# Batched Wo rows and residual assembly in small steps around V and Wo, x blocks transposed by DMA, VectorE side work in the Wo stretch

## The chip, the cores and the metric

One core of a Trainium2 chip. The metric is device time in microseconds (us), lower is better. Before the change: 902.95 us, median of 3 runs (901.86 to 905.41). A *step* below is the time from the first exponential of one recurrent segment to that of the next, read from the timeline; there are 63 such intervals between 64 segments. *Position* 0 to 3 is the step's number modulo 4, and four steps make one block of 128 rows of x.

## The reference

Layer norm, then attention with a recurrent memory over 64 segments of 32 rows (32 heads, 8 memory rows made anew by each segment), a residual, then layer norm and a gMLP mixer with a second residual.

```python
for s in range(n_seg):                       # 64, each needs the memory of the one before
    h = concat([mem, xs], axis=1)            # 8 + 32 rows
    q, k, v = h @ Wq, h @ Wk, h @ Wv         # 32 heads of 128
    p = softmax(where(mask, q @ k.T * scale, -1e9))
    o = (p @ v) @ Wo
    mem, out_s = o[:, :M], o[:, M:]
h  = x + concat(outs)
h2 = h + gmlp(layernorm(h))                  # w_in, w_sp (2048 x 2048), w_out
```

## The kernel before

The last 8 rows of each segment don't depend on the order in which the memory runs (the name `X` marks them): their Q, K and V for all segments of a chunk are made in *extra groups*, one group in each of steps 0 to 47, and their output rows are multiplied by Wo apart, four segments at a time (`WoX`). The parts that the change touches, in the program order of one step; `late` is work that is emitted early in the next step, behind the memory rows:

```python
for s in range(NSEG):
    j4, rb = s % 4, s // 4
    QK(s, QKP[0], (0, 1))
    if s > 0:
        mem_out(s - 1, 1)                    # memory rows back into hT
        for f in late: f()                   # <- evictions, statistics, ...
    # ... QK pieces, ScalarE evacuation, VectorE stream transposes, scores, exp, V ...
    for f in xs[:2]: f()                     # extra group, first half of its matmuls
    PV_half(s, 0); PV_half(s, 1)
    for f in xs[2:4]: f()                    # second half
    if j4 == 3 and rb > 0:
        F_group(rb - 1, WXB)                 # assembles 128 rows of the residual
        WoX_scatter(rb - 1, WXB)
    # ... cT evictions ...
    if j4 == 3 and rb > 0:
        F_add(rb - 1, WXB)
    Wo(...); part_evac(...); mem_out(s, 0); mask_dve()     # cut
    late += xs[4:]                           # extra group's eviction, VectorE
    if j4 == 1 and 2 <= rb + 2 < RB:
        ln_inplace(0)                        # x block rb+2: statistics, rstd, apply
    if j4 == 2 and 2 <= rb + 2 < RB:
        xT(0, FBK)                           # four PE transposes
        late.append(lambda rb=rb: ring_copy(rb + 2, FBK))  # ScalarE
    if s + 1 < NSEG and s >= 3:
        WoX_mm((s + 1) // 4 - 1, (j4 + 1) % 4)             # 8 matmuls in every step
        if j4 == 2:
            late.append(lambda rb=rb: WoX_evac(rb - 1))    # ScalarE
    if j4 == 0 and rb >= 2:
        xn2_apply(rb - 2, rb % 2); xn2_store(rb - 2, rb % 2)
    if s == 3 * CK:                          # step 48
        sp(lambda e: e.dma_start(w_in2, winr[:, :, FH:F]), ...)   # 896 KB for the tail
```

Every odd step also has a DMA transpose of 64 rows of w_sp and its 256 KB store (`wT_piece`). All DMA is issued by one queue, SP, in program order (in the trace before, the 896 KB load went out at 567.68 us, behind the store of `xn2` at 567.30 that stands ahead of it).

## Time and profile before

| stretch | us |
|---|---|
| start, to the first exponential | 58.3 |
| step 0 | 15.4 |
| steps 1 to 15 | 155.8 |
| steps 16 to 47 | 331.3 |
| steps 48 to 62 | 152.3 |
| rest: last segment and gMLP tail | 190.7 |

From the profile page of the kernel before: busy time of each engine, and shares of the chain of waits by engine.

```profile
PE 870.1 (96%) x22506; PEld 537.7 (59%) x22513; DVE 499.6 (55%) x1231; ACT 451.9 (50%) x1274; POOL 156.4 (17%) x403
...
PE 88%; DVE 7%; issue 2%; ACT 1%; POOL 1%; DMA 0%; SPq 0%; ACTq 0%
```

The shortest steps of each position in steps 16 to 47 are 9.96, 10.45, 10.43 and 10.39 us. At the end of position 1 the chain of waits of the kernel before leaves PE (columns: start, duration, engine, tile, line, count):

```profile
327.97 0.10 PE f_ps L648 x8
...
328.26 0.53 DVE f_ps L509
328.80 0.60 DVE f_st L353
...
329.42 0.19 DVE f_mv L354
...
329.69 0.23 POOL f_rs L355
...
330.00 0.58 POOL f_rs L357
...
330.60 0.41 DVE f_xn L363
331.01 0.60 DVE f_arena L416
331.61 0.36 DVE f_QT L491
...
332.71 0.83 PE f_ps L573 x12
```

L509 is the mask copy, L353 to L363 the normalisation of an x block with its detour over GpSimd, L416 the extra group's eviction. The stream transpose of Q (L491) that PE will need stands behind all of it in VectorE's order.

In the last 16 segments there are no extra groups, and the chain of the kernel before leaves PE ahead of PV and ahead of Wo (L627):

```profile
561.89 0.69 DVE f_V_sb L584
562.58 0.30 DVE f_E_sb L559
562.89 0.34 DVE f_V_sb L584
...
563.98 0.30 ACT f_cT L612
...
564.33 1.80 PE f_ps L627 x56
```

One step later, the same chain has a piece that no engine explains: "issue", time in which PE waited for nothing that the profile shows.

```profile
574.28 0.29 PE f_ps L627 x3
574.57 1.40 issue
575.97 1.69 PE f_ps L627 x53
```

### The profile page before, as it was taken

What the parts mean: (1) busy time and instruction counts of PE and PEld (TensorE: products, weight loads), DVE (VectorE), ACT (ScalarE), POOL (GpSimd) and SP (SyncE); (2) the same over time, 40 slices, a digit from 0 to 9 for tenths busy, and PEclk for the clock granted to TensorE, in tenths of its full rate; (3) what the DMA queues carried; (4) which work ended last, traced back from release to release, by engine and by line L of the source; (5) the groups of instructions that cost most, each with busy time, mean ns of one, the idle gap of its engine ahead of it and who ended that gap; (6) DMA issues with size and microseconds to landing.
All of it is one profiled execution on the core that took longest, in us unless ns stands there. A gap on an engine that the chain in (4) does not pass through costs nothing.

```text
span 903.8 us, 48903 instructions
## 1 busy us (share of the span) xinstructions
PE 870.1 (96%) x22506; PEld 537.7 (59%) x22513; DVE 499.6 (55%) x1231; ACT 451.9 (50%) x1274; POOL 156.4 (17%) x403
## 2 busy tenths in 40 slices
PE   7989999999999999999999999899999999999997
PEld 6665666566666666666666666556566544434443
DVE  3435556566666656566666666555655554543343
ACT  2335566555566655666555666556665655300000
POOL 1501111121211211112212112111111122100000
PEclk9999999999999999999999999999999999999999
DMA  9971211322203020312113120404123590022101
GB/s 327 377 211 45 62 54 42 71 62 57 72 27 68 22 71 21 76 34 55 53 42 58 35 69 22 123 26 93 41 48 63 176 275 1 1 99 76 59 12 37
DMA packets 99586, 71.50 MB, mean 79 GB/s; under 512 B 62248, under 2 KB 84912, under 8 KB 99376
## 3 DMA queue, kind: packets, MB, share of 16 engines
q1 hardware_dynamic: 99376, 68.32, 27.6%
q8 instruction: 178, 2.92, 1.3%
q14 instruction: 32, 0.26, 0.1%
HBM read 39.46 MB, written 18.61 MB: 64 GB/s over the span
## 4 chain that ended last, share of the span: by engine, by line
PE 88%; DVE 7%; issue 2%; ACT 1%; POOL 1%; DMA 0%; SPq 0%; ACTq 0%
PE f_ps L472 21%; PE f_ps L627 13%; PE f_ps L573 11%; PE f_ps L1012 11%; PE f_ps L405 7%; PE f_ps L424 3%; PE f_ps L592 3%; PE f_ps L677 3%; PE f_ps L974 3%; PE f_ps L1005 3%; PE f_ps L1083 3%; PE f_ps L539 2%; DVE f_V_sb L584 2%; PE f_ps L598 1%; PE f_ps L519 1%
## 5 line engine op out<-in xcount | busy, mean ns | idle before, releaser
L472 PE MATMUL f_ps<-f_arena,f_hT 128*32 128x512 bf16 (+1 forms) x5120 | 239.9, 337 | 0.1
L472 PEld LDWEIGHTS f_ps<-f_arena,f_hT 128*32 128x32 bf16 x5120 | 125.8, 96 | 94.2 <-ACT f_hT L656 23.0
L483 ACT ACTIVATE f_Tst<-f_ps 128x512 bf16<-128x512 f32 (+1 forms) x320 | 148.5, 512 | 56.7 <-PE f_ps L472 47.1
L573 PE MATMUL f_ps<-f_arena,f_hT 128*32 128x256 bf16 (+1 forms) x3072 | 143.5, 308 | 0.5
L627 PE MATMUL f_ps<-f_arena,f_cT 128*32 128x256 bf16 x4096 | 133.5, 275 | 6.4 <-ACT f_cT L612 4.6
L563 POOL TENSOR_TENSOR f_E_sb<-f_R_sb,f_E_sb 128x64 bf16<-128x64 f32 x128 | 48.0, 375 | 409.3 <-ACT f_R_sb L555 409.3
L627 PEld LDWEIGHTS f_ps<-f_arena,f_cT 128*32 128x32 bf16 x4096 | 95.6, 96 | 29.2 <-ACT f_cT L612 11.5
L491 DVE STREAM_TRANSPOSE f_QT<-f_Tst 128x256 uint32<-128x256 uint32 x128 | 56.9, 445 | 89.5 <-ACT f_Tst L483 89.5
L1012 PE MATMUL f_ps<-f_arena 128*128 128x512 bf16 x448 | 103.0, 384 | 2.4 <-DVE f_arena L1018 1.6
L639 ACT ACTIVATE f_part<-f_ps 128x256 bf16<-128x256 f32 x128 | 49.0, 383 | 92.7 <-PE f_ps L627 92.7
L584 DVE TENSOR_SCALAR f_V_sb<-f_ps 128x512 bf16<-128x512 f32 (+1 forms) x128 | 70.6, 551 | 41.1 <-PE f_ps L573 41.1
L614 DVE TENSOR_SCALAR f_cT<-f_ps 128x160 bf16<-128x160 f32 (+1 forms) x192 | 61.0, 374 | 39.3 <-PE f_ps L598 39.3
L1012 PEld LDWEIGHTS f_ps<-f_arena 128*128 128x128 bf16 x448 | 43.9, 99 | 57.2 <-DVE f_arena L1018 2.6
L573 PEld LDWEIGHTS f_ps<-f_arena,f_hT 128*32 128x32 bf16 x3072 | 68.8, 96 | 14.5 <-ACT f_Tst L483 1.8
L612 ACT ACTIVATE f_cT<-f_ps 128x160 bf16<-128x160 f32 (+1 forms) x192 | 53.0, 349 | 40.0 <-PE f_ps L598 40.0
L405 PE MATMUL f_ps<-f_hTe,f_arena 128*128 128x128 bf16 x1024 | 70.4, 223 | 0.1
L491 DVE STREAM_TRANSPOSE f_KT<-f_Tst 128x128 uint32<-128x128 uint32 (+1 forms) x192 | 63.8, 338 | 3.1
L405 PEld LDWEIGHTS f_ps<-f_hTe,f_arena 128*128 128x128 bf16 x1024 | 58.9, 99 | 9.2 <-issue 7.1
L551 ACT ACTIVATE f_R_sb<-f_ps 128x160 f32<-128x160 f32 x128 | 38.8, 303 | 35.8 <-PE f_ps L544 35.8
L654 DVE CAST f_hT<-f_ps 128x16 bf16<-128x16 f32 x63 | 11.0, 175 | 78.2 <-PE f_ps L648 78.2
L1018 DVE TENSOR_TENSOR f_arena<-f_ps,f_arena 128x512 f32<-128x512 f32 x28 | 19.3, 691 | 59.5 <-PE f_ps L1012 59.5
L559 DVE TENSOR_TENSOR f_E_sb<-f_R_sb,f_E_sb 128x160 bf16<-128x160 f32 x128 | 45.6, 356 | 0.0
(103 smaller groups left out, 1089.5 us busy)
## 6 DMA issues: line engine op xcount, KB each, us to landing
wT_d<-f_wst SPq DMA_DIRECT2D x32, 256.0 KB, 2.5
f_arena<-wT_d SPq DMA_DIRECT2D x32, 256.0 KB, 4.3
f_arena<-in_A_Wq_dram SPq DMA_DIRECT2D x4, 1024.0 KB, 8.6
f_arena<-in_A_Wv_dram SPq DMA_DIRECT2D x4, 1024.0 KB, 14.3
f_arena<-in_A_Wk_dram SPq DMA_DIRECT2D x4, 1024.0 KB, 14.5
f_arena<-in_A_Wo_dram SPq DMA_DIRECT2D x4, 1024.0 KB, 8.5
f_Vx<-vext_d SPq DMA_DIRECT2D x64, 64.0 KB, 2.7
f_xn<-in_A_x_dram SPq DMA_DIRECT2D x17, 128.0 KB, 2.5
```

The costliest lines, as they stand in the source:

```text
L405: pe(lambda e, h=h, dc=dc, hh=hh: e.matmul(ps[:, bank, hh * 128:(hh + 1) * 128], lhsT=ws[:, dc, h * DH:(h + 1) * DH], rhs=hTe[:, ck % 3, d ...
L472: pe(lambda e, dc=dc, c=c, rhs=rhs: e.matmul(ps[32 * c:32 * c + 32, bank, 0:32 * nh], lhsT=hT[:, sl, dc, :], rhs=rhs, start=(dc == 0), sto ...
L483: act(lambda e: e.activation(out=st_.rearrange("p (hp i r) -> p hp i r", i=32, r=2), in_=ps[:, bank, 0:64 * np_].rearrange("p (hp r i) -> ...
L491: dve(lambda e: e.transpose(out=dst, in_=src), reads=tok, writes=[(nm, b, k) for k in halves(b, p0, np_)])
L563: pool(lambda e: e.tensor_tensor(out=ev, in0=rv, in1=ev, op=ALU.mult), reads=[("R", b), ("Ex", b)], writes=[("Ex", b)])
L573: pe(lambda e, dc=dc, c=c, c0=c0: e.matmul(ps[32 * c:32 * c + 32, bank, 0:w], lhsT=hT[:, sl, dc, :], rhs=w_v[:, dc, c0:c0 + w], start=(dc ...
L584: dve(lambda e: e.tensor_scalar(out=dst, in0=src, scalar1=VSC, scalar2=None, op0=ALU.mult), reads=[PB(bank)], writes=tok)
L612: act(lambda e: e.activation(out=dst, in_=src, func=ACT.Copy, scale=UNSC), reads=[PB(PVB[c])], writes=tok)
L614: dve(lambda e: e.tensor_scalar(out=dst, in0=src, scalar1=UNSC, scalar2=None, op0=ALU.mult), reads=[PB(PVB[c])], writes=tok)
L627: pe(lambda e, h=h, g=g, i=i, b=b, c=c: e.matmul(ps[32 * g:32 * g + 32, bank, 0:d1 - d0], lhsT=cTh[:, i, 8:40], rhs=w_o[:, h, d0:d1], star ...
L639: act(lambda e: e.activation(out=part[:, s % 8, d0:d1], in_=ps[:, bank, 0:d1 - d0], func=ACT.Copy), reads=[PB(bank)], writes=[("part", s % ...
L1012: pe(lambda e: e.matmul(ps[:, bank, 0:TB], lhsT=z2[:, sc, fb * 128:(fb + 1) * 128], rhs=wTb[tb % 2][:, :, sc, :], start=(sc == 0), stop=(s ...
```

## The change

Its intent: take the x transposes off PE, take VectorE's normalisation and evictions out of the way of the stream transposes, and move the WoX, F and scatter matmuls to where PE has room.

```diff
+    def x_flip(j, i, dst, tok):                  # store to DRAM, DMA transpose back
+        sp(lambda e: e.dma_start(xs_d[i], t), ...)
+        sp(lambda e: e.dma_start_transpose(out=dst, in_=xs_d[i]), ...)
+    def ring_fill(rb):                           # VectorE copy into hT
...
+        nw1, nw4 = ((1, 1, 0, 0)[j4], (2, 2, 0, 2)[j4]) if s < 3 * CK else ((4, 4, 0, 0)[j4], 0)
+        if j4 == 3 and rb > 0:
+            WoX_scatter(rb - 1, WXB)
+        for f in wq[:nw1]:                       # WoX in pieces of 4 matmuls, ahead of PV
+            f()
...
-        if j4 == 3 and rb > 0:
-            F_group(rb - 1, WXB)
-            WoX_scatter(rb - 1, WXB)
...
         if j4 == 3 and rb > 0:
             F_add(rb - 1, WXB)
+            late += xs[4:]
+            late.append(lambda rb=rb: h_done(rb - 1))
+        else:
+            for f in xs[4:]:                     # extra group's eviction, ahead of Wo
+                f()
...
-        late += xs[4:]
+        if j4 == 0 ...: late.append(lambda: ln_stats(0))
+        if j4 == 0 ...: late.append(lambda rb=rb: ring_fill(rb + 1))
         if j4 == 1 and 2 <= rb + 2 < RB:
-            ln_inplace(0)
+            late.append(lambda rb=rb: (ln_apply(0), x_flip(0, rb, ...)))
-        if j4 == 2 and 2 <= rb + 2 < RB:
-            xT(0, FBK)
-            late.append(lambda rb=rb: ring_copy(rb + 2, FBK))
-        if s + 1 < NSEG and s >= 3:
-            WoX_mm((s + 1) // 4 - 1, (j4 + 1) % 4)
+        if s + 1 < NSEG:
+            if j4 == 3:
+                wq.extend(... 8 pieces of WoX_mm ...)
+            elif j4 == 2 and rb > 0:
+                F_group(rb - 1, WXB)
+            for f in wq[:nw4]:                   # behind Wo
+                f()
...
-        if j4 == 0 and rb >= 2:
-            xn2_apply(rb - 2, rb % 2)
-            xn2_store(rb - 2, rb % 2)
+        if j4 == 1 and rb >= 2: late.append(... xn2_apply, xn2_store ...)
```

(Cuts and shortened conditions are marked by dots.)

More of the change, by code (lines that the diff above doesn't have):

```diff
@@ L255, in fast_path @@
     h_d = nc.dram_tensor("h_d", [RB, 128, D], BF, kind="Internal").ap()
+    xs_d = nc.dram_tensor("xs_d", [RB + 1, 128, D], BF, kind="Internal").ap()
     wT_d = nc.dram_tensor("wT_d", [S // 64, 128, RB, 64], BF, kind="Internal").ap()
@@ L378, in slot @@
         return s % NSLOT
+    def x_flip(j, i, dst, tok):
+        t, rd = xbuf(j)
+        sp(lambda e: e.dma_start(xs_d[i], t), reads=rd, writes=[("xs", i)])
+        sp(lambda e: e.dma_start_transpose(out=dst, in_=xs_d[i]), reads=[("xs", i)], writes=[tok])
+    def ring_fill(rb):
+        src = xn[:, 1, :].rearrange("p (dc s c) -> p s dc c", dc=DC, s=4, c=SEG)[:, :, :, 0:XM]
+        s0 = slot(4 * rb)
+        dve(lambda e: e.tensor_copy(out=hT[:, s0:s0 + 4, :, M:32], in_=src), reads=[("xn", 1)], writes=[("hTx", rb % 3)])
     def ring_copy(rb, bank):
@@ L671, in load_h, with WoX_mm @@
         sp(lambda e: e.dma_start(hbuf[:, rb % 2, :], xr[:, rb, :]), writes=[("h", rb % 2)])
-    def WoX_mm(rb, qr):
-        for bg in range(8):
+    def WoX_mm(rb, qr, bgs=range(8)):
+        for bg in bgs:
             b, g = bg // 4, bg % 4
@@ L821, in fast_path @@
     lastop = {}
+    wq = []
     qx_copy(0)
@@ L834, in fast_path @@
         if s == 1:
-            load_xe(3, 1)
+            load_xe(3, 7)
         QK(s, QKP[0], (0, 1))
@@ L884, in fast_path @@
             lastop["x"] = em.by_eng["pool"][-1]
+        late = []
+        nw1, nw4 = ((1, 1, 0, 0)[j4], (2, 2, 0, 2)[j4]) if s < 3 * CK else ((4, 4, 0, 0)[j4], 0)
[3 more added lines that the diff above has]
+            f()
+        del wq[:nw1]
         xs = gx.pop(0) if gx else []
-        late = []
         for f in xs[:2]:
@@ L912, in fast_path @@
         part_evac(s, OB2, OC, D)
-        if j4 == 3 and rb > 0:
-            late.append(lambda rb=rb: h_done(rb - 1))
-        late += xs[4:]
+        if j4 == 0 and 2 <= rb + 2 < RB:
+            late.append(lambda: ln_stats(0))
+        if j4 == 0 and 2 <= rb + 1 < RB:
+            late.append(lambda rb=rb: ring_fill(rb + 1))
         if j4 == 1 and 2 <= rb + 2 < RB:
-            ln_inplace(0)
+            late.append(lambda rb=rb: (ln_apply(0), x_flip(0, rb, xn[:, 1, :].rearrange("p (dc c) -> p dc c", dc=DC), ("xn", 1))))
+        if s == 2:
+            late.append(lambda: ln_stats(7))
         if s == 3:
-            ln_inplace(1)
-        if j4 == 2 and 2 <= rb + 2 < RB:
-            xT(0, FBK)
-            late.append(lambda rb=rb: ring_copy(rb + 2, FBK))
-        if s == 5:
-            xT(1, FBK)
-            late.append(lambda: xe_copy(3, FBK))
-        if s + 1 < NSEG and s >= 3:
-            WoX_mm((s + 1) // 4 - 1, (j4 + 1) % 4)
-            if j4 == 2:
-                late.append(lambda rb=rb: WoX_evac(rb - 1))
-        if s + 1 == NSEG:
+            late.append(lambda: (ln_apply(7), x_flip(7, RB, hTe[:, 0, :, :], ("hTe", 0))))
+        if j4 == 1 and rb >= 2:
+            late.append(lambda rb=rb: (xn2_apply(rb - 2, rb % 2), xn2_store(rb - 2, rb % 2)))
+        if j4 == 1 and rb > 0:
+            late.append(lambda rb=rb: WoX_evac(rb - 1))
+        if s + 1 < NSEG:
+            if j4 == 3:
+                wq.extend(lambda rb=rb, k=k: WoX_mm(rb, k // 2, range(4 * (k % 2), 4 * (k % 2) + 4)) for k in range(8))
+            elif j4 == 2 and rb > 0:
+                F_group(rb - 1, WXB)
+            for f in wq[:nw4]:
+                f()
+            del wq[:nw4]
+            assert not wq or j4 in (0, 3)
+        else:
             for f in late:
```

## The prediction

> **What bounds it now.** The page gives PE 96% busy, and the chain of waits is 88% PE. The 64 recurrent steps take 654.8 us of the 903.8 (first to last step's first exponential, timeline). [...]nearly all slices read 9, yet step lengths by position in a block of four, steps 16 to 47, are 9.96, 10.46, 10.45 and 10.39 us.
>
> - Position 1 alone has a chain that leaves PE, for VectorE and GpSimd (statistics 0.60, aggregate 0.19, GpSimd 0.23 and 0.58, apply 0.41, then the 0.60 eviction of the extra QK/V group), which hold up the first Q/K stream transposes. Cost 0.49 us.
> - Position 2: four PE transposes of x (0.33 us in the chain), and two extra ScalarE evictions (0.48, 0.60) ahead of the first Q/K evacuation (about 0.15 more).
> - Position 3: F and scatter matmuls, 8 in about 0.54 us, 0.43 net.
> - Each step from 3 on also has 8 WoX matmuls (0.43 us) between Wo and QK.
>
> The last 16 steps have no extra groups: the chain runs V evictions and normalisation on VectorE (0.69, 0.30, 0.34) and a 0.30 cT eviction on ScalarE, so PE idles about 0.4 us before PV and about 0.3 before Wo. These steps still take 9.95 us.
>
> **What changes.**
>
> - Removed: the PE transposes (13 blocks x 0.33 = 4.3 us), the ring evictions on ScalarE, and the normalisation chain waiting on itself in front of the stream transposes: about 0.5 us in each of 13 blocks = 6.5 us. The position 2 ScalarE delay, 0.15 x 12 = 2 us.
> - Moved: WoX and F/scatter matmuls, count unchanged, to position 3, 0 and 1 after Wo or between V and PV. For steps 16 to 47 PE work per block becomes 4 x 9.53 + 1.73 (32 WoX) + 0.43 (8 F/scatter) = 40.3 us against 41.2 to 41.7: 1.0 us per block, more in steps 0 to 15 where PV already waits a little. In the last 16 steps they land where PE idled: about 0.4 us a block, plus the transposes, 2 us in all. The extra eviction moves to VectorE's idle Wo stretch.
> - Added: 13 stores of 128 KB (similar ones land in 2.2 us), 13 DMA transposes (similar: 3.1 us), 12 VectorE copies[...]. Steps of slack hide them.[...]
>
> Sum: about 6 us in steps 0 to 15, 7 in 16 to 47, 2 at the end: 15 us. The gMLP tail (184 us) is unchanged.
>
> **Prediction: 888 us, 883 to 894 (8 in 10).** Chances: faster by over 2% 0.27, within 2% 0.72, slower by over 2% 0.01.
>
> **Right if:** position 1's chain is PE only; no PE transposes before the tail; steps near 10.15, 10.15, 9.75, 10.15 us in steps 16 to 47; ScalarE idle grows; VectorE copies of x stay off the chain. **Wrong if:** Wo with no WoX behind it exposes the memory-row eviction (0.1 us a step at least in steps 48 to 63); the 16 matmuls before PV exceed the hole in the last 16 steps; VectorE work queued after the mask copy delays the stream transposes again; or PE instruction-fetch waits (4.1 and 1.4 us in this trace) move.

## The result, and the profile after

892.8 us median of 4 runs (891.3 to 895.6), beside 902.4 us of the kernel before (4 runs). The ratio is 0.989, 95% interval 0.986 to 0.993: faster by about 1.1%, inside the predicted range. A ratio is the mean time of one kernel's fast runs over that of the other's of the same rounds, so it is not quite the ratio of the medians quoted. The unaltered changed kernel was run twice more as a control: 893.3 us against 907.1 (ratio 0.985, interval 0.982 to 0.988) and 894.8 against 904.1 (0.988, interval 0.983 to 0.992). The changed kernel repeats better than the kernel before, whose medians in the four sessions were 902.4, 906.4, 907.1 and 904.1; the prediction set out from its fast end.

From the page of the changed kernel:

```profile
PE 854.8 (96%) x22453; PEld 524.2 (59%) x22453; DVE 504.3 (57%) x1245; ACT 449.2 (50%) x1259; POOL 156.3 (18%) x403
...
PE 94%; DVE 3%; issue 2%; ACT 1%; DMA 0%; POOL 0%; SPq 0%
```

The share of PE in the chain rose from 88 to 94%, GpSimd left it and VectorE's share went from 7 to 3%: in steps 16 to 47 of this trace the chain is PE and 1.3 us of "issue", so the stalls that the prediction named there are gone. The chain of waits of the changed kernel at the end of position 1, the place shown of before at 328 us:

```profile
480.52 1.66 PE f_ps L638 x56
482.18 0.05 PE f_ps L659 x8
482.23 0.24 PE f_ps L638 x8
482.47 0.43 PE f_ps L688 x8
482.90 0.43 PE f_ps L483 x7
483.33 0.04 PE f_ps L659 x7
483.36 3.11 PE f_ps L483 x72
486.47 0.09 PE f_ps L530 x16
```

It is PE from Wo (L638) over the memory rows (L659), WoX (L688) and QK (L483) to the scores (L530). The shortest steps of the positions in steps 16 to 47 are now 10.07, 10.07, 9.77 and 10.07 us, 39.98 a block against 41.23 before (each sum from the four shortest steps). But not all steps are so short. By stretch, in us, in the traces of the kernel before and of three runs of the changed one (its first, and the two controls):

| stretch | before | changed, three traces |
|---|---|---|
| step 0 | 15.4 | 12.6, 11.0, 11.0 |
| steps 1 to 15 | 155.8 | 153.2, 152.8, 154.1 |
| steps 16 to 47 | 331.3 | 323.8, 327.5, 327.2 |
| steps 48 to 62 | 152.3 | 153.7, 151.6, 150.4 |
| all steps | 654.8 | 643.2, 643.0, 642.8 |

The steps gained 11.6 to 12.0 us where 15 were predicted. That gain is flattered: the trace of the kernel before is of a run of 905.5 us, 2.5 above its median, and its step 0 holds a 4.1 us piece of "issue" with 3.41 us at half clock after it. Eight blocks of 39.98 would make 319.8 us for steps 16 to 47; the three traces stand 4.0 to 7.7 above that, and in the kernel before the same difference was 1.5 (331.3 less 8 x 41.23). So part of what the order gained came back as irregular waits.

In the last 16 segments the chain still leaves PE. V evictions (L595) hold 6.2 us of it in this trace, where they held 15.6 before, and cT evictions 4.5 (3.6 before). One piece is new: with no WoX behind Wo, the eviction of the memory rows (L665) lies between Wo and QK, 0.19 us in 11 of the 15 steps.

```profile
556.36 0.10 PE f_ps L659 x7
...
556.48 0.19 DVE f_hT L665
...
556.71 0.61 PE f_ps L483 x7
```

The largest irregular wait is in step 48. The chain of waits of the changed kernel there:

```profile
549.29 0.86 PE f_ps L688 x16
550.15 0.13 PE f_ps L603 x3
550.28 2.15 issue
552.42 0.26 PE f_ps L603 x13
...
553.38 2.98 PE f_ps L638 x52
```

PE stopped for 2.15 us between two matmuls of the same group (L603), and then the Wo matmuls (L638) took 2.98 us, where they take 1.66 above. Busy time and granted clock (PEclk, the third value from the end) of the changed kernel in stretches of that step show why:

```profile
550.00:552.40 2.40, 0.28 (x7) 0.10 (x3) 0.00 (x0) 0.00 (x0) 0.57 (x2) 1.00 0.11 22
552.40:554.00 1.60, 1.22 (x52) 0.98 (x56) 0.91 (x3) 0.83 (x3) 0.00 (x0) 0.57 0.46 174
554.00:556.00 2.00, 2.00 (x44) 1.55 (x40) 0.04 (x1) 0.38 (x1) 0.40 (x1) 0.50 0.48 98
```

After the wait PE ran at half clock; the trace's clock records put it at 552.61 us for 3.41 us. Step 48 took 13.58 us, 3.5 more than the typical 10.1 of its position in the last 16 segments.

What does PE wait for? "issue" only says that no semaphore explains it. The trace also records DMA packets of kind "instruction": 178 packets of 16,384 bytes on one queue. Each "issue" wait of PE in the recurrent part was held against the last such packet that ended before the wait did:

```
wait of PE (us)     last instruction packet   wait ends after packet's end
 59.96 to  62.14     59.54 to  60.86          1.28
156.53 to 156.88    154.43 to 155.35          1.52
216.26 to 217.15    214.78 to 215.71          1.44
389.74 to 390.20    387.00 to 388.82          1.38
550.28 to 552.42    549.90 to 550.95          1.48
582.28 to 582.89    580.39 to 581.44          1.46
all 18 waits of the changed kernel             1.28 to 1.56
all 9 waits of the kernel before               1.21 to 1.67
```

Packets come about every 4 us (median 3.90 us from start to start in the trace before, 3.89 in the changed kernel's), so a wait that had nothing to do with them would end anywhere from 0 to 4 us after one. All 27 end 1.2 to 1.7 us after, and so do 263 of the 264 waits in the other twelve traces (1.16 to 1.93 us). From this I take it that PE was waiting for its own instructions. The kernel before has 178 such packets too, and PE ran 45,019 matmuls and weight loads in it: about 253 a packet, an estimate from these two counts, with every packet taken as PE's, of the instructions that one brings (a *block* below). Between 56 and 730 us either trace has 164 packets, so 9 waits before and 18 after mean that most blocks came without one; the waits there add up to 6.8 us before and 10.4, 8.9 and 9.6 us in the three traces of the changed kernel. "Fetch waits" below are this sum: PE's idle gaps over 60 ns that are put down to "issue".

This sum is a floor. The trace draws a matmul of Wo 273 ns long, though 56 of them start within 1.6 us, so a late start shows as a gap only beyond the end of the one before. Against the starts of PE's instructions in the shortest step of the same position, the first trace stands thus: of the 4.0 us that steps 16 to 47 take above the shortest, 3.6 arise 1.1 to 1.75 us after the end of a packet, where the gaps show 1.3; in the first control, 6.8 of 7.6, where they show 3.5. So nearly all of that excess goes with the fetch.

In step 48 the packet before this one had started at 543.02; the next started only at 549.90, 6.9 us later. Between 546 and 550 us DMA moved 308 GB/s. The timelines of the SP queue, first of the kernel before, then of the changed one, show what had moved (start, duration of the issue):

```profile
567.68 0.50 SPq L940 DMA_DIRECT2D f_arena<-in_B_w_in_dram  x1
```

```profile
542.92 1.81 SPq L963 DMA_DIRECT2D f_arena<-in_B_w_in_dram  x1
...
545.32 1.27 SPq L732 DMA_TRANSPOSE f_wst<-in_B_w_sp_dram  x1
```

The line of the 896 KB load of w_in isn't in the diff. Before, SP reached it only in step 49, because the store of `xn2` ahead of it in SP's order waited for VectorE until 567.3 us; there it came with the 1.40 us piece of "issue" shown above, in a step 49 of 11.51 us. The change moved that store elsewhere, and the load went out 25 us earlier, ahead of step 48's exponentials: SP issued it at 542.92 us, and the first of these started at 547.22.

### The profile page after: what moved, and what is told of

Its sections match the earlier page's. It is cut to its first block, busy times and chain, and to the rows that moved or that the text cites. A ratio compares the mean times of both kernels' runs of the same rounds, so it can differ in the third digit from the quotient of the medians.

```text
span 890.5 us, 48841 instructions
## 1 busy us (share of the span) xinstructions
PE 854.8 (96%) x22453; PEld 524.2 (59%) x22453; DVE 504.3 (57%) x1245; ACT 449.2 (50%) x1259; POOL 156.3 (18%) x403
## 4 chain that ended last, share of the span: by engine, by line
PE 94%; DVE 3%; issue 2%; ACT 1%; DMA 0%; POOL 0%; SPq 0%
PE f_ps L483 26%; PE f_ps L638 14%; PE f_ps L584 12%; PE f_ps L1035 11%; PE f_ps L416 7%; PE f_ps L435 3%; PE f_ps L688 3%; PE f_ps L997 3%; PE f_ps L1028 3%; PE f_ps L603 3%; PE f_ps L1106 3%; PE f_ps L550 2%; PE f_ps L530 1%; PE f_ps L609 1%; DVE f_V_sb L595 1%
## 5 line engine op out<-in xcount | busy, mean ns | idle before, releaser
L483 PE MATMUL f_ps<-f_arena,f_hT 128*32 128x512 bf16 (+1 forms) x5120 | 241.3, 337 | 1.5 <-issue 0.5
L483 PEld LDWEIGHTS f_ps<-f_arena,f_hT 128*32 128x32 bf16 x5120 | 125.1, 96 | 96.4 <-ACT f_hT L667 22.9
L638 PE MATMUL f_ps<-f_arena,f_cT 128*32 128x256 bf16 x4096 | 134.7, 275 | 9.2 <-ACT f_cT L623 6.2
L638 PEld LDWEIGHTS f_ps<-f_arena,f_cT 128*32 128x32 bf16 x4096 | 92.8, 96 | 34.2 <-ACT f_cT L623 13.1
L595 DVE TENSOR_SCALAR f_V_sb<-f_ps 128x512 bf16<-128x512 f32 (+1 forms) x128 | 70.6, 552 | 41.4 <-PE f_ps L584 41.4
L584 PEld LDWEIGHTS f_ps<-f_arena,f_hT 128*32 128x32 bf16 x3072 | 69.2, 96 | 14.7 <-issue 2.2
L502 DVE STREAM_TRANSPOSE f_KT<-f_Tst 128x128 uint32<-128x128 uint32 (+1 forms) x192 | 65.7, 343 | 4.2
L543 ACT ACTIVATE f_E_sb<-f_ps 128x224 bf16<-128x224 f32 x128 | 45.1, 353 | 0.0
```

Of the source, the lines that this page charges most:

```text
L483: pe(lambda e, dc=dc, c=c, rhs=rhs: e.matmul(ps[32 * c:32 * c + 32, bank, 0:32 * nh], lhsT=hT[:, sl, dc, :], rhs=rhs, start=(dc == 0), sto ...
L502: dve(lambda e: e.transpose(out=dst, in_=src), reads=tok, writes=[(nm, b, k) for k in halves(b, p0, np_)])
L584: pe(lambda e, dc=dc, c=c, c0=c0: e.matmul(ps[32 * c:32 * c + 32, bank, 0:w], lhsT=hT[:, sl, dc, :], rhs=w_v[:, dc, c0:c0 + w], start=(dc ...
L595: dve(lambda e: e.tensor_scalar(out=dst, in0=src, scalar1=VSC, scalar2=None, op0=ALU.mult), reads=[PB(bank)], writes=tok)
L638: pe(lambda e, h=h, g=g, i=i, b=b, c=c: e.matmul(ps[32 * g:32 * g + 32, bank, 0:d1 - d0], lhsT=cTh[:, i, 8:40], rhs=w_o[:, h, d0:d1], star ...
```

## The experiments

Theory A: the predicted gain is real as a sum of PE work and stalls removed, and what is missing is PE waiting for its instructions behind DMA traffic. Rivals are named with each run. The first four kernels ran on one chip (before: 906.4 us), the other eight on another (before: 907.1 and 904.1 us). All are correct except the one made wrong.

### One part undone: x transposed on PE again

```diff
-  ring_fill(rb + 1) on VectorE; x_flip(...) after ln_apply(0)
+  if j4 == 2 ...: xT(0, FBK); late.append(lambda rb=rb: ring_copy(rb + 2, FBK))
```

> The changed kernel with one part undone: x blocks transposed by PE in position 2 and evicted by ScalarE again, batching and VectorE placement kept. Theory A (gain is the sum of PE work and stalls removed; the excess over it is PE waiting for its instructions behind DMA traffic): position 2 goes from 9.77 to about 10.10 us, 13 x 0.33 = 4.3 us on the sum of the shortest steps (626.7 to about 631), fetch waits fall a little from 10.4 us, so 1 to 4 us slower than the changed kernel (892.8), about 895. Rival B (the DMA transposes cost what was missing from the predicted gain): as fast as the changed kernel or faster, fetch waits under 6 us.

Measured: 894.0 us, ratio 0.986 (interval 0.981 to 0.990). The shortest step of position 2 went from 9.77 to 10.18 us, the others stayed at 10.07. From the groups of PE's instructions of this kernel in steps 16 to 31, the transposes are back:

```profile
L374 PE MATMUL f_ps<-f_ident,f_xn 128*128 128x128 bf16 x16 | 1.6, 222 | 0.0
```

Fetch waits were 8.2 us. So the order pays 0.4 us a block for PE transposes, as theory A had it, but the whole kernel was no slower than the changed one by a margin that the runs resolve (0.986 against 0.985 to 0.989), and all its steps took 645.3 us against 643. By that difference the transposes on DMA would be worth about 2 us, not the 4.3 of their PE work, but this compares one trace with three, and fetch waits alone move steps 16 to 47 by 3.7 us between traces of the same kernel: the worth in time is not resolved. Rival B is not supported: waits did not fall under 6.

### One part undone: WoX in every step again

```diff
-  pieces of WoX ahead of PV and behind Wo; F_group in position 2, scatter ahead of PV
+  WoX_mm((s + 1) // 4 - 1, (j4 + 1) % 4) in every step; F_group and scatter ahead of Wo in position 3
```

> The changed kernel with one part undone: 8 WoX matmuls after Wo in every step, F and scatter before Wo in position 3, as before. Theory A: PE work per block is the same, so the block of four in steps 16 to 47 stays at 40.0 us within 0.2 (10.4 in position 3, less elsewhere), and the last 16 steps go from about 39.6 to 39.8 a block: 1 us slower in all, about 894. Rival (batching is what pays): block back to 40.5 or more, 6 us slower in all, about 899.

Measured: 896.9 us, ratio 0.989 (0.984 to 0.994). The shortest steps are 9.96, 9.96, 9.96 and 10.39, 40.27 a block, 0.3 more than the changed kernel's 39.98; steps 16 to 47 sum to 327.4 us, the same as two of the three traces of the changed kernel. In the last 16 segments steps went back to 9.95 us each. The bound of 0.2 us was missed by 0.1: four matmuls ahead of PV cost a step 0.11 us (10.07 less 9.96), not the 0.21 that their piece of the chain shows. They start 1.89 us into the step; the extra group's matmuls, which stand ahead of PV in both kernels, start only at 2.00 where they follow V directly, so half of the cost falls into a hole that was there. Why they start no earlier is not shown. By time it lies between theory and rival, and its ratio is that of the recorded result (0.989), so the runs don't resolve it.

### One part undone: the extra group's eviction late again

```diff
-            for f in xs[4:]: f()     # ahead of Wo
+            late += xs[4:]           # behind the mask copy, in the next QK stretch
```

> The changed kernel with one part undone: the eviction of the extra group goes back behind the mask copy in the QK stretch in all positions. Theory A: VectorE has about 2 us between the mask copy and the first stream transpose, and the queued work (eviction 0.6, statistics 0.8[...]) just fits: position 1's chain stays PE only, at most 0.2 us a block, under 2 us in all, 893 to 895. Rival (the place of the eviction is what pays): VectorE back in position 0 or 1's chain by 0.4 us or more a block, 5 us or more slower, 898 or more.

Measured: 898.3 us, ratio 0.990 (0.985 to 0.994). The time is in the rival's range and the mechanism is not: the shortest block is 39.98 us, the same as the changed kernel's. VectorE's timeline at the end of position 0 in this kernel (in brackets: idle time before, and its releaser):

```profile
480.77 0.68 DVE L427 CAST f_arena<-f_ps 128x512 bf16<-128x512 f32 x1
481.37 0.69 DVE L354 BATCH_NORM_STATS2 f_st<-f_xn 128x6 f32<-128x512 bf16 x1
482.09 0.18 DVE L355 BATCH_NORM_AGGREGATE f_mv<-f_st 128x2 f32<-128x6 f32 x1
482.19 0.23 DVE L389 COPY f_hT<-f_xn 128x384 bf16<-128x384 bf16 x1
482.83 0.45 DVE L502 STREAM_TRANSPOSE f_QT<-f_Tst 128x256 uint32<-128x256 uint32 x1 [0.42 <-ACT f_Tst L494]
```

The eviction (L427), statistics and copy (0.23 us) all fit, and VectorE still idles 0.42 us for ScalarE before the stream transpose. Fetch waits were 13.4 us here, 3.6 of them in step 0, which took 15.6 us. This profile is of the slowest of the four runs, and its span is 8.7 us above the changed kernel's first: 5.6 in the steps, of which 3.0 in step 0 (that wait, with 6.8 us at half clock around its end), 1.3 before them and 1.8 after. So fetch waits are part of the extra time; why they should be more in this kernel stays open. The control is on another chip, and by ratio the kernel is no slower than the recorded result (0.989). Moving this eviction ahead of Wo, one part of the change, is thus not shown to pay.

### The suspected cost taken away: no w_sp transposes (wrong result)

```diff
-        if s % 2 == 1 and s // 2 < NWT:
-            wT_piece(s // 2)          # 32 DMA transposes and stores of 256 KB
```

The tail loads w_sp untransposed, in pieces of the same size, hence the wrong result.

> The changed kernel without the 32 DMA transposes of the spatial weight and their stores; the tail loads the weight untransposed, so the result is wrong on purpose. Theory A (PE's instruction fetch is held up behind bursts of DMA, mostly these): the fetch waits of PE between 56 and 730 us fall from 10.4 to 3 us or less, no half-clock stretch, and it is 7 to 12 us faster than the changed kernel (881 to 886). Rival C (the waits come from the change's own DMAs, or from PE issuing faster than instructions can be brought): waits stay at 8 us or more, at most 3 us faster.

Measured: 888.8 us, ratio 0.981 (0.977 to 0.985). Waits of PE in this kernel (us in total, times, longest):

```profile
PE f_ps L603 <- issue: 2.9, 4, 1.0
PE f_ps L435 <- issue: 1.7, 2, 1.5
...
PE f_ps L638 <- issue: 1.2, 4, 0.6
```

Fetch waits were 7.0 us, not 3 or less, and all 17 of them again end 1.27 to 1.59 us after an instruction packet. Theory A was right in kind and too strong in size: the transposes are one source of traffic in front of the fetch, worth about 4 us of time (888.8 against 893, the latter from other sessions), not the only one. Step 48, which had no transpose beside its load here, still took 11.66 us, with a wait of 0.96 us. Step 9 is telling: 11.0 to 11.8 us in the changed kernel's traces, 9.95 here.

### The control, and three edits against it

> The changed kernel unaltered, on the chip that the next three run on, as their control. 892 to 896 us, 0.988 of before; PE's fetch waits in the recurrent stretch 8 to 13 us, as in its first profile (10.4) and the variants' (7.0 to 13.4).

Measured: 893.3 us, ratio 0.985; fetch waits 8.9. As expected, but for the ratio, which was a little lower since the kernel before was slower on this chip.

The last 16 segments refilled:

```diff
-  ((4, 4, 0, 0)[j4], 0)             # pieces ahead of PV in steps 48 on
+  ((2, 2, 0, 0)[j4], 0)             # and two more between PV and Wo
```

> The changed kernel with one size changed: in the last 16 steps, positions 0 and 1, half of the WoX pieces (8 matmuls) stay ahead of PV and half go between PV and Wo, where PE waits 0.38 us for the ScalarE eviction of cT. Theory (the 16 matmuls ahead of PV overfill a hole of about 0.4 us): these positions go from 10.09 and 9.98 us to 9.76 like the other two, 8 steps x 0.22 to 0.33 = 2.2 us off the sum of steps, about 2 us faster than the control. Rival (the steps are set by the chain through VectorE and ScalarE alone): no change over 0.5 us.

Measured: 893.5 us, ratio 0.986, no change in time against the control. Position 1 of the last 16 fell to 9.77 us in all its later steps (9.98 in the control), so there the 16 matmuls ahead of PV did overfill the hole. Position 0, which was to fall too, did not: 9.95 to 10.42 us in its later steps, 10.11 to 10.29 in the control; why is open. Step 48 of this profile took 14.7 us, with one fetch wait of 3.5 us and 3.41 us at half clock after it, and swallowed the gain.

The w_sp transposes in halves:

```diff
-  dma_start_transpose(wst[:, :, :], B_w_sp[64 rows])                    # odd steps
+  dma_start_transpose(wst[:, :, 32*k:32*k+32], B_w_sp[32 rows])         # every step
```

> The changed kernel with each 64-row DMA transpose of the spatial weight cut into two of 32 rows, one in each step, same bytes. Theory D (fetch waits come from long DMA bursts ahead of the fetch): waits fall by 2 us or more from the control's, 1 to 4 us faster. Theory E ([...]since they stayed at 7.0 us with no such transposes at all): within 2 us of the control in waits and time.

Measured: 893.4 us, ratio 0.985, fetch waits 9.0: the same as the control. Theory D as stated fails for these transposes: the same bytes in shorter bursts buy nothing. Theory E, whose first clause is cut, puts the waits down to where the fetches fall in the program against PE's dense stretches.

Fetch boundaries shifted by 128 PE instructions, about half a block by the estimate above:

```diff
+    for k in range(64):      # while PE waits for the first x block
+        pe(lambda e: e.matmul(ps[0:32, 5, 0:8], lhsT=ident[:, 0:32], rhs=ident[:, 0:8], start=True, stop=True), ...)
```

> The changed kernel with 64 tiny matmuls (128 PE instructions[...]) put where PE waits for the first x block, so that all later fetches fall 128 instructions earlier in the program; nothing else changes. Theory E: the steps with waits move (step 31's repeated 1.0 us excess, seen with and without the weight transposes, goes), the sum of waits changes by 2 us or more either way. Theory D: the same steps wait, sum within 2 us.[...]

Measured: 892.8 us, ratio 0.984 (0.980 to 0.987), fetch waits 9.8 against the control's 8.9. Step 9 lost its excess (9.95 us) and step 5 gained one (11.09 against 10.13 in the control), which speaks for theory E's first half: where a block ends mattered to where PE waited. The sum did not change by 2 us. Step 31, which I had named, took 10.07 us in the control as well, so it told nothing. Since step 9 waits neither when boundaries are shifted nor when the w_sp traffic is gone, it seems to take both, traffic and a boundary in a bad place; with one trace each that is not settled.

### The moved load

> The changed kernel unaltered, as control for the next three on their chip: about 893 us, 0.985 to 0.990 of before. Step 48 takes 12.4 to 13.6 us instead of 10.1 (13.58 and 12.41 in the two profiles so far), with a fetch wait of PE of about 2 us and a stretch of half clock after it.

Measured: 894.8 us, ratio 0.988; step 48 took 11.9 us with two waits of 1.4 us in sum, the longer 0.96, and no half clock, which the first control (12.41 us) had not shown either.

Eight small loads in place of the large one:

```diff
-        if s == 3 * CK:
-            sp(lambda e: e.dma_start(w_in2, winr[:, :, FH:F]), ...)                 # 896 KB
         if 0 <= s - 3 * CK - 1 < 8:
             xn2T_dma(s - 3 * CK - 1, free0)
+            dc, c0 = (s - 3 * CK - 1) // 2, (s - 3 * CK - 1) % 2 * HFW
+            sp(lambda e: e.dma_start(w_in2[:, dc, c0:c0 + HFW], winr[:, dc, FH + c0:FH + c0 + HFW]), ...)
```

> The changed kernel with the one 896 KB load of the second half of w_in, issued at the end of step 48, replaced by eight loads of 112 KB at the ends of steps 49 to 56. Theory (this load, brought forward by the change from 567.7 to 542.9 us on the queue, starves PE's instruction fetch in step 48): step 48 falls to 10.7 us or less, no fetch wait over 1 us and no half clock there, and none of steps 49 to 56 gains over 0.3 us on average: 2 to 3 us faster than the control. Rival (the weight transpose of that step or the step's dense stretch is the cause): step 48 stays over 11.5 us.

Measured: 889.6 us, ratio 0.983 (0.978 to 0.988), 5.2 us below the control's median; the runs of both overlap (886.2 to 892.7 and 890.6 to 896.4). Step 48 took 10.46 us. The chain of waits of this kernel at the place where the changed one stopped for 2.15 us:

```profile
549.08 0.86 PE f_ps L688 x16
549.95 0.20 PE f_ps L603 x16
...
550.76 1.80 PE f_ps L638 x56
```

The same WoX and PV matmuls follow each other without a wait, and Wo takes 1.80 us. Steps 49 to 56, where the small loads run, took 79.5 us together and 79.3 in the control, so they did not pay for it, and fetch waits fell from 9.6 to 6.4 us. All traces agree: step 48 took 11.12 to 14.70 us in the ten traces of the changed kernel and its variants that issue the whole load there, and 9.98 to 10.46 in the three that do not (this one, and the two below). The rival, the transpose of that step, is out: without it (no w_sp transposes) the step was long, and here it is short with it. The gain in time is larger than the 2 to 3 us expected; the two traces differ by 4.8 us in their steps (638.0 and 642.8), of which 0.9 is in steps 48 to 62 and 2.3 and 2.2 in steps 1 to 15 and 16 to 47, where the edit does nothing. So 1 to 3 us are shown to come from the load (1.5 in step 48 here, 3.1 against the first trace); the rest may be the scatter of fetch waits from run to run.

The same load, whole, one step later:

```diff
-        if s == 3 * CK:
+        if s == 3 * CK + 1:
             sp(lambda e: e.dma_start(w_in2, winr[:, :, FH:F]), ...)
```

> The changed kernel with the 896 KB w_in load issued whole, one step later (end of step 49 in the program, near where it ran before the change). Theory: the wait follows the load: step 48 falls to 10.7 us or less, and step 49 or 50 takes 1.4 to 3.5 us more; total within 1.5 us of the control, up to 2 faster if no half-clock stretch follows, as in the kernel before (1.4 us wait, none). Rival: step 48 keeps its wait.

Measured: 893.2 us, ratio 0.987. Step 48 fell to 9.98 us and step 49 rose from 9.76 to 10.67, with a fetch wait of 0.76 us: the wait followed the load. Its size was smaller than expected. The total is the control's within noise, so the earlier issue only moved a wait that the kernel before had too; what pays is the smaller loads.

Both edits together:

> Both edits that should pay: the eight small w_in loads, and WoX in the last 16 steps half ahead of PV and half ahead of Wo. Steps 48 to 62 near 9.77 to 9.95 us, so 4 to 5 us faster than the control, about 889, the fastest of all; if only the load pays, as drip.

(Edit: the two diffs above, small loads and the refilled last 16 segments.) Measured: 887.7 us, ratio 0.980 (0.976 to 0.984), 7.1 us below the control, the fastest of all kernels here, and correct; its six runs (884.4 to 890.1) all lie below the control's six. It beats both the kernel before and the changed one; against the small loads alone the 2 us are not resolved. Position 1 of the last 16 fell to 9.77 to 9.92 us; position 0 again missed what was expected (10.08 to 10.49).

## Why the prediction was right or wrong, point by point

The time of the recorded result, 892.8 us, was within the range of 883 to 894; the two controls gave 893.3 and 894.8, the second just above it. The gain was smaller than the 15 us forecast: 1.1 to 1.5% by the three ratios, 9.3 to 13.8 us by the medians. That it stayed in the range is in part luck: the order came out better than forecast, in steps 16 to 47 about 10 us by the shortest steps where 7 were predicted, and the fetch waits worse.

- **Position 1's stall** was right. The chain there is PE only, and the shortest step of position 1 is 10.07 us with 0.11 us of added WoX, where it had been 10.45. No run puts the normalisation back, so this rests on the two chains and on what is left over: of the 1.25 us a block, undoing the transposes shows 0.41 and undoing the batching 0.29, and the remaining 0.55 is near the stall's 0.49.
- **PE transposes** were right in size as PE work: 0.41 us a block when put back (10.18 less 9.77). The 0.15 us put down to ScalarE was not ScalarE's: in position 2 of the kernel before, the transposes start at 5.58 us into the step where WoX starts at 5.45 in the other positions, and all of the 0.47 us that the step is longer has arisen when QK starts (6.35 against 5.88). In time the 0.41 us is not resolved (645.3 against 643 us of steps).
- **PE work per block.** I predicted 40.3 us; the shortest steps give 39.98. The step that erred is "4 x 9.53 + 1.73 + 0.43": matmuls ahead of PV were counted at full cost and cost half.
- **"About 6 us in steps 0 to 15, 7 in 16 to 47, 2 at the end: 15 us."** This is the sum that failed in size. Measured: steps 0 to 15 5.4, 7.4 and 6.1 us, which looks like the 6 predicted but is luck: 2.8 to 4.4 of it is in step 0 alone, where the trace before happened to hold its 4.1 us wait, and steps 1 to 15 gained only 1.7 to 3.0; steps 16 to 47 7.5, 3.8 and 4.1; the end -1.4, 0.7 and 1.9. It assumed that every step would be as long as its kind's shortest. The order did become about 1.25 us a block shorter, and fetch waits took back part: 6.8 us of them before, 8.9 to 10.4 after. This was the last item of the list of what could go wrong.
- **The end.** I had not seen that moving the store of `xn2` lets SP reach the 896 KB load a step earlier, although the order of SP's queue was in the trace. It put waits into step 48 (1.4 to 2.15 us in all, and in the first trace half clock after them), in place of the 1.40 us that step 49 had before. The 16 matmuls ahead of PV did exceed the hole, as the prediction feared: 10.09 and 9.98 us in positions 0 and 1, 9.76 in the others. The other fear for this stretch came true as well: the memory-row eviction is exposed, 0.19 us in 11 of 15 steps.
- **Added DMA.** Stores landed in 1.9 us (2.2 estimated), transposes in 4.1 rather than 3.1, VectorE copies took 0.23 us. None is on the chain of the steps.
- **"ScalarE idle grows"** was wrong: in the 63 steps it fell from 263.1 to 254.2, 254.0 and 252.9 us, since the steps became shorter by more than ScalarE's work did.
- **Half clock** came with some of the waits; the prediction does not mention it. Fetch waits of 4.08 us (the kernel before), 3.5 (refilled segments), 2.15 (the changed kernel), 1.44 (late eviction) and 1.23 (halved transposes) were each followed by 3.41 us at half clock, while waits of 2.81 us (halved transposes), 2.18 (the changed kernel, step 0) and 1.40 (the kernel before) were not. So the length of one wait alone did not decide it; what did is open.
- **The time set out from** was a fast session of a kernel whose medians range over 4.7 us here.

What stays open: how fetch waits divide among the sources of DMA traffic, PE's rate and the place of the block boundaries; why the kernel with the late eviction had more of them; and what position 1's stall is worth when it alone is put back.

## What to carry to other kernels

When an engine is nearly full and its gaps are put down to nothing, hold them against the instruction packets of the trace: this tuned, fully unrolled kernel waited 6.4 to 13.4 us a run, it seems for its own instructions, 2.15 us of it beside one 896 KB load and a transpose. When you move one DMA in an in-order queue, look at what stood behind it and now goes out early (here 25 us), and try cutting a bulk load that nothing needs soon into small ones (here it paid for one load of 896 KB; halving the transposes did not). Forecast from the shortest steps what an order can reach, and take the scatter of the longer ones as a cost that may grow as slack is removed.
